# VectorE's middle steps as a loop, and a new order for the last two pairs of K tiles

## The chip, the cores and the metric

The kernel runs on one core of a Trainium2 chip. It uses TensorE (PE, matmul), VectorE (DVE), ScalarE (ACT), GpSimd (POOL, here only for a few set-up instructions and for passing on news of landed transfers) and SyncE (SP, which issues the transfers). The metric is the time of one execution on the device, in microseconds, lower being better. The median of three runs of the kernel before is 2525.35 us (2525.32 to 2525.47).

## The reference, cut to what matters

One token is decoded: attention of one query per head over a long cache (32 heads, 65536 keys, head size 128, bfloat16), a small gated feed-forward block, and a gate that mixes both.

```python
q = (x @ wq).reshape(B, Sq, H, Dh).transpose(0, 2, 1, 3)      # x: 1 x 1 x 512, H = 32, Dh = 128
scores = jnp.einsum("bhqd,bhkd->bhqk", q, k_cache) * (Dh ** -0.5)   # Sk = 65536
p = softmax(scores)
o = jnp.einsum("bhqk,bhkd->bhqd", p, v_cache)
a = o.transpose(0, 2, 1, 3).reshape(B, Sq, H * Dh) @ wo
b = (silu(x @ w_gate) * (x @ w_up)) @ w_down
g = sigmoid((x * gate_w).sum(-1, keepdims=True))
return g * a + (1 - g) * b
```

The K cache and the V cache have 512 MiB each, and every byte of them is read once.

## The kernel before

Keys are handled in *tiles* of 128 x 128 keys: partition p holds 128 keys of 128 numbers, 4 MB in all. A head has four K tiles and four V tiles (G = 4), so there are N = 128 tiles of each, in M = 64 *pairs* (two tiles, 8 MB, half a head). On chip there are two buffers for K pairs (`K_bufs`) and one for a V pair (`V_buf`).

A step m works on K pair m and, two pairs behind it, on V pair m - 2:

- VectorE (`vector_step`) multiplies each K tile by the query, laid out over all partitions (`product`), and adds halves of the 128 columns: 128 to 64, to 32, to 16 (`add_halves`). The last add writes `T_sb`. It also folds finished scores out of PSUM into `S_sb` (`fold`), takes the head's maximum per partition (`row_max`), the maximum over partitions (`top_of`) and the reciprocal of the softmax sum (`weight`).
- TensorE (`tensor_step`) finishes the sum over the remaining 16 columns by matmuls with a unit matrix that accumulate in PSUM, four columns each (`scores`: 16 columns are 4 matmuls, 32 are 8, 64 are 16). It multiplies probabilities by V (`values`, 32 matmuls per tile), turns the head's output (`head_turn`), spreads the query of the next head, turns the maxima (`max_turn`) and sums the exponentials (`total`). Its program already has the middle steps as a loop, in which it waits for *credits*: semaphores that others raise by one and that it lowers again.
- ScalarE (`scalar_step`) takes the exponentials into `P_sb`, spreads queries and scales the head's output.
- SP (`sync_step`) issues the loads: V pair m - 1 when the values of the V pair ahead of it are done (semaphore `pe_V`), for odd pairs as two tiles, and then K pair m + 2 when the scores of pair m are done (`pe_S`). All its transfers go through one queue, in the order in which they are issued.

The first two pairs are written out by hand in `prologue`, 64 columns wide. VectorE, ScalarE and SP have one instruction after the other for all 64 pairs; each waits for counts that only rise, remembered in `seen` so that no count is waited for twice. Order within an engine is the order in which the instructions are written.

At the end there is no more K to load, and the four last V tiles (124 to 127) take the place of what has been used: 124 and 127 lie in halves of the K buffers, 125 and 126 in `V_buf`. The output matrix wo comes in pieces, the first 16 heads early and the rest (`LATE_CUTS`) behind the last V tile. `sync_end` issues all that, `tensor_end` has TensorE's order: scores of the last pair 32 wide, straight from the K buffer (`scores_direct`), values of V tiles 122 to 127, and between them the projection with wo (`project`, two matmuls per head). The last eight columns of the last V tile go straight into `head_turn`'s accumulator. `vector_end` and `scalar_end` copy one half of the output each, and `sync_out` sends it.

Of the kernel before, what the change touches and what calls it, by code (L numbers as in the profile page):

```python
# [10 lines left out]
P = 128  # L11
NB = 128
PAIR = 2 * NB
QUAD = 4

FIRST = 64
WIDTH = 16
LAST = 32

# [22 lines left out]
def kernel(  # L42
# [53 lines left out]
    out_sb = sb("out_sb", [1, D], bf16)  # L96
    qT, rg = sb("qT", [P, H]), sb("rg", [P, H])
    oT = sb("oT", [P, H], bf16)
# [34 lines left out]
    def v_view(n):  # L133
# [8 lines left out]
    )  # L142
    ac, ac_q, dv, dv_top, dv_max, dv_rg = (
        Events(nc, n) for n in ("ac", "ac_q", "dv", "dv_top", "dv_max", "dv_rg")
    )
    x_in, gw_in, wq_in, kb_in, wg_in, wu_in, wd_in, vA_in, vB_in = (
        Events(nc, n, 16)
        for n in ("x_in", "gw_in", "wq_in", "kb_in", "wg_in", "wu_in", "wd_in", "vA_in", "vB_in")
    )
# [9 lines left out]

    seen = {}  # L160

    def wait(engine, events, value):
        key = id(engine), id(events)
        if seen.get(key, 0) < value:
            engine.wait_ge(events.sem, value)
            seen[key] = value
# [33 lines left out]
    def load_k(m):  # L200
        if m in (0, M - 1):
            for n in range(2):
                load_tile(K_half[m % 2][n], A_k_cache, 2 * m + n, (k_in[m % 2], kb_in)[n])
        else:
            load_pair(K_bufs[m % 2], A_k_cache, m, k_in[m % 2])

    def sync_step(m):
        load_v(m - 1)
        if m + 2 < M:
            wait(sync, pe_S, 2 * m + 2)  # L210
            load_k(m + 2)

    def sync_end():
        wait(sync, pe_S, N - 2)
        load_wo(0, EARLY)
        load_tile(v_view(N - 4), A_v_cache, N - 4, v4_in)
        for n in (N - 3, N - 2, N - 1):
            if n < N - 1:
                wait(sync, pe_V, n - 2)
            else:  # L220
                wait(sync, pe_S, N)
            cuts = LAST_CUTS if n == N - 1 else HALVES
            for events, a, b in zip(end_in[n], cuts[:-1], cuts[1:]):
                load_tile(v_view(n), A_v_cache, n, events, a, b)
        for a, b in zip(LATE_CUTS[:-1], LATE_CUTS[1:]):
            load_wo(a, b)

    def sync_out():
        wait(sync, dv, dv.n)
        wait(sync, ac, ac.n)  # L230
        out_in(sync.dma_start(out=out[0], in_=out_sb))
        sync.sem_inc(done.sem, 1)
# [20 lines left out]
    marks = {}  # L253

    def product(n):
        K = K_half[n // 2 % 2][n % 2]
        q = q_sb[n // G % 2]
        q_rep = bass.AP(tensor=q.tensor, offset=q[:, :].offset, ap=[list(q[:, :].ap[0]), [0, NB], [1, Dh]])
        m = n // 2

        if m in (0, M - 1) and n % 2:
            wait(dve, kb_in, 16 if m == 0 else 32)
        else:
            wait(dve, k_in[m % 2], 16 * (m // 2 + 1))
        wait(dve, ac_q, n // G + 1)
        return dv(dve.tensor_tensor(out=K, in0=K, in1=q_rep, op=ALU.mult))  # L266

    def add_halves(n, width, last, out=None, ahead=None):
        K = K_half[n // 2 % 2][n % 2]
        half, mark = Dh // 2, last  # L270
        while half >= width:
            wait(dve, dv, mark)
            to = K[:, :, 0:half]
            if half == width and ahead is not None:
                fold(ahead)
            if half == width and out is not None:
                wait(dve, pe_S, n)
                to = out
            ins = dve.tensor_tensor(out=to, in0=K[:, :, 0:half], in1=K[:, :, half : 2 * half], op=ALU.add)  # L279
            if half == width and out is not None:  # L280
                ins.then_inc(c_S[n % 2], 1)
            else:
                mark = dv(ins)
            half //= 2
        marks["K", n] = mark

    def fold(n):
        h, g = divmod(n, G)
        wait(dve, pe_S, n + 1)
        return dv(dve.tensor_reduce(  # L290
            out=S_sb[h % 2][:, g * NB : (g + 1) * NB], in_=S_ps[n % 2], axis=AXIS.X, op=ALU.add
        ))

    def row_max(h, folded):
        wait(dve, dv, folded)
        dv_max(dve.tensor_reduce(out=m_sb[:, 0:1], in_=S_sb[h % 2], axis=AXIS.X, op=ALU.max))  # L296

    def top_of(h):
        wait(dve, pe_m, 2 * h + 1)
        dv_top(dve.tensor_reduce(out=top[:, 0:1], in_=mT, axis=AXIS.X, op=ALU.max))  # L300

    def weight(h, t):
        wait(dve, pe_t, t)
        if h < H - 1:
            wait(dve, dv, dv(dve.tensor_reduce(out=tsum[:, 0:1], in_=tot, axis=AXIS.X, op=ALU.add)))
            total = tsum[:, 0:1]
        else:
            total = tot[:, 0:1]
        wait(dve, dv, dv(dve.reciprocal(recip[:, 0:1], total)))
        dv_rg(dve.tensor_tensor(out=rg[:, h : h + 1], in0=recip[:, 0:1], in1=gval, op=ALU.mult))  # L310

    def vector_step(m):
        h, b = divmod(m, MH)
        width, to = (WIDTH, T_sb) if m < M - 1 else (LAST, None)
        last = product(2 * m)
# [9 lines left out]
        if b == 1:  # L325
            row_max(h, fold(2 * m + 1))

    def vector_end():
        top_of(H - 1)
        weight(H - 1, M - 1)  # L330
        wait(dve, pe_x, 5)
        dv(dve.tensor_copy(out=out_sb[:, :HD], in_=a_ps[0]))  # L332

# [4 lines left out]
    def query(h, credit):  # L338
# [7 lines left out]
        wait(act, pe_q, pe_q_after(2 * h - 1) if h else 1)  # L346
        ac_q(copy(q_sb[h % 2], qb))

# [4 lines left out]
    def head_diag(h, credit):  # L353
        m = 2 * h + 1
        wait(act, dv_max, h + 1)
        wait(act, pe_m, m - 1)
        ins = copy(diag, ident_f, m_sb[:, 0:1])
# [25 lines left out]
    def head_out(h, src):  # L383
        wait(act, dv_rg, h + 1)
        if h >= GROUPED:
            return copy(oT[:, h : h + 1], src, rg[:, h : h + 1])
        g, part = divmod(h, QUAD)
        A = P // QUAD
        for j in range(QUAD):
            ins = copy(  # L390
                oT[part * A : (part + 1) * A, g * QUAD + j : g * QUAD + j + 1],
                src[j * A : (j + 1) * A, :],
                rg[j * A : (j + 1) * A, h : h + 1],
            )
# [31 lines left out]
    def scalar_end():  # L426
# [12 lines left out]
        wait(act, pe_x, 6)  # L439
        ac(copy(out_sb[:, HD:], a_ps[1]))  # L440

# [4 lines left out]

    def scores(n, src, width):
        for c in range(0, width, QUAD):
# [3 lines left out]
            )  # L452
        pe_S(ins)

    def scores_direct(n, width):
        wait(pe, dv, marks["K", n])
        scores(n, K_half[n // 2 % 2][n % 2], width)

    def query_spread():
        pe_q(pe.matmul(qb, lhsT=ones_b, rhs=q_diag, start=True, stop=True))  # L460

    def max_turn():
        pe_m(pe.matmul(mT, lhsT=ones_f, rhs=diag, start=True, stop=True))  # L463

# [30 lines left out]
    def prologue():  # L495
# [35 lines left out]

        add_halves(0, FIRST, product(0))
        scores_direct(0, FIRST)
        wait(dve, x_in, 16)
# [8 lines left out]
        fold(0)  # L543
        add_halves(1, FIRST, last)
        scores_direct(1, FIRST)
        wait(dve, ac, marks["eg2"])
# [18 lines left out]
        marks["eg"] = ac(act.activation(out=eg, in_=gu_sb[:, :FT], func=ACT.Exp, scale=-1.0))  # L565
        wait(sync, pe_S, 2)
        load_k(2)

        last = product(2)
        fold(1)  # L570
        add_halves(2, FIRST, last)
        scores_direct(2, FIRST)
        wait(dve, ac, marks["eg"])
# [24 lines left out]
        fold(2)  # L598
        add_halves(3, FIRST, last)
        scores_direct(3, FIRST)  # L600
        wait(sync, pe_S, 4)
        load_k(3)
        row_max(0, fold(3))
        head_diag(0, False)
        wait(pe, ac, marks["diag", 0])
        max_turn()


    def tensor_step():
# [4 lines left out]
        take(c_S[0])  # L614
        scores(0, T_sb, WIDTH)
        take(c_q)
# [3 lines left out]
        take(c_S[1])  # L620
        scores(1, T_sb, WIDTH)
        take(c_o)
        head_turn()
        take(c_m)
        max_turn()

    def tensor_end():
        scores_direct(N - 2, LAST)
        take(c_P)
        total()  # L630
        take(c_V)
        pe_V(values(P_sb, V_half[0], 0, NB, True, False))
        take(c_V)
        lower = P_sb[:, NB:]
        values(lower, V_half[1], 0, NB // 2, False, False)
        scores_direct(N - 1, LAST)
        values(lower, V_half[1], NB // 2, 3 * NB // 4, False, False)
        wait(pe, ac, marks["diag", H - 1])
        max_turn()
        pe_V(values(lower, V_half[1], 3 * NB // 4, NB, False, True))  # L640
        wait(pe, wo_in[0], 16)
# [18 lines left out]
        for j in range(NB - TURNED, NB):  # L660
# [3 lines left out]
            )  # L664
        wait(pe, ac, marks["O_last"])
        head_turn(opens=False)
        for a, b in zip(LATE_CUTS[:-1], LATE_CUTS[1:]):
            wait(pe, wo_in[a], 16)
            if b == H:
                project(a, H - 1)  # L670
# [5 lines left out]
    with tc.tile_critical():  # L676
        prologue()
        for m in range(2, M):
            vector_step(m)
            scalar_step(m)  # L680
# [3 lines left out]
        sync_end()  # L684
        scalar_end()
        vector_end()
        sync_out()
        with pe.Fori(0, M - 3):
            tensor_step()
# [38 lines left out]
```

## Time and profile before

| | |
|---|---|
| median of 3 runs | 2525.35 us |
| the profiled execution: time / span | 2523.84 us / 2522.0 us |
| DMA: bytes, mean rate | 1087.85 MB, 431 GB/s |
| busy: PE / VectorE / ScalarE | 55% / 88% / 7% of the span |
| TensorE's mean granted clock | 0.731 |
| product of a K tile (line 266), 128 times | 8.69 us each |
| add to 64 columns / to 32 / to 16 (line 279) | 4.42 / 2.29 / 1.22 us |
| fold of a tile (line 290) | 0.69 us |
| values matmul (line 470), 3968 in the middle steps | 0.42 us each, mean |

The span runs from the first to the last instruction of the profiled execution; the 1.84 us around it belong to the execution's own time. Times in the views count from the span's start. A line such as `DVE K_buf L266 <- DMA K_buf: 148.7, 57, 5.6` says that VectorE stood idle ahead of instructions of line 266 until a transfer into a K buffer landed, 148.7 us in total, 57 times, 5.6 us at most. In the timeline a row has its start, its length, the engine, the line, the operation, what it writes and reads, and in brackets the engine's idle time ahead of it. The view of DMA issues gives, for each kind of transfer, how many, their size and the median time from issue to landing.

### The profile page before, as it was taken

The page shows a single profiled execution, that of the slowest core. Times are in us where ns is not written, and L with a number is a line of the kernel's source. Part 1 is how long each engine was busy: PE and PEld are TensorE (multiplying, and loading weights), DVE is VectorE, ACT ScalarE, POOL GpSimd, SP SyncE. Part 2 cuts the span into 40 slices and gives each one's busy share as a digit, 9 for nine tenths or more (in the row PEclk, how much of TensorE's full clock was granted, in tenths as well). Part 3 has the DMA queues.
Part 4 walks back from the last instruction along what each step waited for, and adds up shares of the span by engine and source line. Part 5 has one row for each costly group of instructions (what it writes and reads, how often), then busy time and mean ns, then how long its engine had stood idle before and what let it go on. Part 6 is the DMA issues. An engine that isn't in the chain of part 4 may idle for free. (4 is left out here: it accounts for less than half of the span.)

```text
span 2522.0 us, 14146 instructions
## 1 busy us (share of the span) xinstructions
PE 1388.8 (55%) x5813; PEld 574.9 (23%) x5813; DVE 2220.4 (88%) x802; ACT 187.2 (7%) x503; POOL 0.7 (0%) x6
## 2 busy tenths in 40 slices
PE   2655654546645465554565454654545555556549
PEld 1222222212212122222222121222212222222214
DVE  5898898988988989889889898898898988988992
ACT  0000000000000000000000000000000000000000
POOL 0000000000000000000000000000000000000000
PEclk9767776767767677676777676776767767677769
DMA  9999999999999999999999999999999999999998
GB/s 414 437 435 433 434 439 429 440 433 432 432 432 434 435 432 437 439 428 439 432 433 432 432 437 432 434 437 434 430 439 433 432 433 433 434 432 435 439 429 348
DMA packets 26854, 1087.85 MB, mean 431 GB/s; under 512 B 3154, under 2 KB 3667, under 8 KB 4947
## 3 DMA queue, kind: packets, MB, share of 16 engines
q1 hardware_dynamic: 26546, 1087.65, 99.7%
q8 instruction: 5, 0.08, 0.0%
q14 instruction: 15, 0.11, 0.0%
q10 hardware_dynamic: 288, 0.00, 0.0%
HBM read 1087.64 MB, written 0.00 MB: 431 GB/s over the span
## 5 line engine op out<-in xcount | busy, mean ns | idle before, releaser
L470 PE MATMUL O_ps<-V_buf,P_sb 128*4 128x512 bf16 x3968 | 1006.7, 418 | 519.6 <-PEq L445 519.3
L266 DVE TENSOR_TENSOR K_buf<-K_buf,q_sb 128x16384 bf16<-128x16384 bf16 x128 | 1112.0, 8688 | 173.5 <-DMA K_buf<-in_A_k_cache_dram 173.5
L279 DVE TENSOR_TENSOR K_buf<-K_buf 128x8192 bf16<-128x8192 bf16 x252 | 849.7, 3372 | 5.3
L470 PEld LDWEIGHTS O_ps<-V_buf,P_sb 128*4 128x4 bf16 x3968 | 353.7, 91 | 1132.4 <-issue 729.9
L449 PE MATMUL S_ps<-T_sb,ident_b 128*128 128x512 bf16 x488 | 156.3, 449 | 240.0 <-PEq L445 240.0
L466 PE MATMUL tot_ps<-rs,ones_f 128*128 128x2 f32 (+1 forms) x126 | 29.1, 300 | 230.7 <-PEq L445 230.7
L290 DVE TENSOR_REDUCE S_sb<-S_ps 128x128 f32<-128x512 f32 x128 | 88.3, 690 | 71.8 <-PE S_ps L449 69.7
L279 DVE TENSOR_TENSOR T_sb<-K_buf 128x2048 bf16<-128x2048 bf16 x122 | 148.8, 1220 | 2.1
L336 ACT ACTIVATE O_sb<-O_ps 4x512 f32<-4x512 f32 x63 | 63.0, 1000 | 1066.0 <-PE O_ps L470 1066.0
L449 PEld LDWEIGHTS S_ps<-T_sb,ident_b 128*128 128x128 bf16 x488 | 41.0, 103 | 335.9 <-issue 311.4
L478 PEld LDWEIGHTS oh_ps<-ident_f,O_sb 4*128 4x128 f32 x504 | 85.9, 253 | 46.6 <-issue 46.1
L478 PE MATMUL oh_ps<-ident_f,O_sb 4*128 4x1 f32 x504 | 90.5, 296 | 6.1 <-PEq L445 5.7
L466 PEld LDWEIGHTS tot_ps<-rs,ones_f 128*128 128x128 f32 x126 | 25.7, 254 | 244.5 <-issue 244.4
L463 PE MATMUL qm_ps<-diag,ones_f 128*128 128x128 f32 x126 | 38.5, 398 | 69.7 <-PEq L445 67.6
L449 PE MATMUL S_ps<-K_buf,ident_b 128*128 128x512 bf16 x80 | 27.6, 515 | 44.0 <-DVE K_buf L279 35.7
L336 ACT ACTIVATE q_sb<-qm_ps 128x128 bf16<-128x128 f32 x32 | 8.9, 278 | 560.5 <-PE qm_ps L460 560.5
L463 PEld LDWEIGHTS qm_ps<-diag,ones_f 128*128 128x128 f32 x126 | 25.1, 249 | 74.1 <-issue 71.0
L336 ACT ACTIVATE oT<-whole_o,rg 32x1 bf16<-32x1 f32 (+1 forms) x115 | 33.8, 294 | 2.0
L399 ACT ACTIVATE whole_o<-oh_ps,half_o 128x1 f32<-128x1 f32 x31 | 8.1, 261 | 317.9 <-PE oh_ps L478 317.9
L368 ACT ACTIVATE P_sb<-S_sb,bias 128x256 bf16<-128x256 f32 x62 | 31.5, 508 | 1.2 <-issue 0.2
L332 DVE CAST out_sb<-a_ps 1x256 bf16<-1x256 f32 x1 | 0.4, 413 | 27.0 <-PE a_ps L487 27.0
L449 PEld LDWEIGHTS S_ps<-K_buf,ident_b 128*128 128x128 bf16 x80 | 9.4, 123 | 60.0 <-DVE K_buf L279 45.0
(60 smaller groups left out, 200.4 us busy)
## 6 DMA issues: line engine op xcount, KB each, us to landing
V_buf<-in_A_v_cache_dram SPq DMA_DIRECT2D x62, 4096.0 KB, 20.4
K_buf<-in_A_k_cache_dram SPq DMA_DIRECT2D x4, 4096.0 KB, 31.4
V_buf<-in_A_v_cache_dram SPq DMA_DIRECT2D x4, 2048.0 KB, 17.6
V_buf<-in_A_wq_dram SPq DMA_DIRECT2D x1, 4096.0 KB, 12.4
K_buf<-in_A_v_cache_dram SPq DMA_DIRECT2D x1, 4096.0 KB, 34.1
K_buf<-in_A_v_cache_dram SPq DMA_DIRECT2D x3, 1024.0 KB, 23.3
K_buf<-in_A_wo_dram SPq DMA_DIRECT2D x1, 2048.0 KB, 24.9
V_buf<-in_B_w_gate_dram SPq DMA_DIRECT2D x1, 1792.0 KB, 54.4
```

Of the source, the lines that this page charges most:

```text
L266: return dv(dve.tensor_tensor(out=K, in0=K, in1=q_rep, op=ALU.mult))
L279: ins = dve.tensor_tensor(out=to, in0=K[:, :, 0:half], in1=K[:, :, half : 2 * half], op=ALU.add)
L290: return dv(dve.tensor_reduce(out=S_sb[h % 2][:, g * NB : (g + 1) * NB], in_=S_ps[n % 2], axis=AXIS.X, op=ALU.add))
L332: dv(dve.tensor_copy(out=out_sb[:, :HD], in_=a_ps[0]))
L336: return act.activation(out=out, in_=in_, func=ACT.Copy, scale=scale)
L368: return act.activation(out=out, in_=S_sb[h % 2][:, b * PAIR : b * PAIR + count], func=ACT.Exp, bias=bias[:, 0:1], scale=scale, accum_out= ...
L399: wait(act, ac, ac(act.activation(out=whole_o[:, 0:1], in_=oh, func=ACT.Identity, bias=half_o[:, 0:1], scale=1.0)))
L449: ins = pe.matmul(S_ps[n % 2], lhsT=ident_b, rhs=src[:, :, c : c + QUAD], start=(c == 0), stop=(c == width - QUAD),)
L463: pe_m(pe.matmul(mT, lhsT=ones_f, rhs=diag, start=True, stop=True))
L466: pe_t(pe.matmul(tot[:, :n], lhsT=ones_f, rhs=rs[:, :n], start=True, stop=True))
L470: ins = pe.matmul(O_ps, lhsT=probs[:, j : j + 4], rhs=view[:, j : j + 4, :], start=(opens and j == start), stop=(closes and j == stop - 4),)
L478: ins = pe.matmul(oh, lhsT=O_sb[:, c * Dh : (c + 1) * Dh], rhs=ident_f[0:4, c : c + 1], start=(opens and c == 0), stop=(c == 3),)
```

## The change

- **A loop on VectorE.** Pairs 2 to 61 become 15 rounds of four pairs (`vector_round`, two heads). Within a round the waits count from the round's start; at its end VectorE waits for what the round's counts must have reached and lowers each semaphore by as much. `own[0]` says which counter VectorE's own instructions raise, in the loop `dv_loop`. Counters that the loop lowers are waited for by VectorE alone, so others get their own: the scores of the hand-written pairs raise `pe_D`, first loads of K raise `ka_in`, `kb_in` and `kc_in`, the first query raises `ac`. `rg` has two columns instead of 32.
- **K loads wait for another event.** SP issues K pair m + 2 after step m's `head_turn` (`pe_o`), where it was after its scores (`pe_S`). ScalarE's `head_diag` no longer waits for `pe_m`.
- **The last two pairs**, 62 and 63, stand outside both loops (TensorE's runs 60 times, not 61), and both are 64 columns wide: one add per tile on VectorE, 16 matmuls per tile on TensorE, where pair 62 was 16 and pair 63 was 32 wide.
- **TensorE's order at the end.** In both last steps the scores of a tile stand ahead of the values of a tile: scores 124, values 120, scores 125, values 121, then scores 126, values 122, scores 127, values 123 in two halves with the max turn between. The last `head_turn` moves behind the first four heads of the 16-to-24 piece of wo, for which TensorE thus waits earlier.

```diff
-        width, to = (WIDTH, T_sb) if m < M - 1 else (LAST, None)
+        width, to = (WIDTH, T_sb) if m < M - 2 else (WIDE, None)
...
+    def vector_round():
+        own[0] = dv_loop
+        for m in range(2, 2 + 2 * MH):
+            vector_step(m)
+        for events, n in ((dv_loop, dv_loop.n), (pe_S, 8), (pe_m, 4), (pe_t, 4), (ac_q, 2), *((k, 32) for k in k_in)):
+            dve.wait_ge(events.sem, n)
+            dve.sem_inc(events.sem, -n)
+        own[0] = dv
...
     def sync_step(m):
         load_v(m - 1)
         if m + 2 < M:
-            wait(sync, pe_S, 2 * m + 2)
+            wait(sync, pe_o, m - 1)
             load_k(m + 2)
 
     def sync_end():
-        wait(sync, pe_S, N - 2)
+        wait(sync, pe_D, 6)
         load_wo(0, EARLY)
...
-                wait(sync, pe_S, N)
+                wait(sync, pe_D, 8)
...
     def head_diag(h, credit):
-        m = 2 * h + 1
         wait(act, dv_max, h + 1)
-        wait(act, pe_m, m - 1)
...
     def tensor_end():
-        scores_direct(N - 2, LAST)
+        lower = P_sb[:, NB:]
         take(c_P)
         total()
+        scores_direct(N - 4)
         take(c_V)
         pe_V(values(P_sb, V_half[0], 0, NB, True, False))
+        scores_direct(N - 3)
+        take(c_q)
+        query_spread()
         take(c_V)
-        lower = P_sb[:, NB:]
+        pe_V(values(lower, V_half[1], 0, NB, False, True))
+        take(c_o)
+        head_turn()
+        take(c_m)
+        max_turn()
+
+        take(c_P)
+        total()
+        scores_direct(N - 2)
+        take(c_V)
+        pe_V(values(P_sb, V_half[0], 0, NB, True, False))
+        scores_direct(N - 1)
+        take(c_V)
         values(lower, V_half[1], 0, NB // 2, False, False)
-        scores_direct(N - 1, LAST)
-        values(lower, V_half[1], NB // 2, 3 * NB // 4, False, False)
         wait(pe, ac, marks["diag", H - 1])
         max_turn()
-        pe_V(values(lower, V_half[1], 3 * NB // 4, NB, False, True))
+        pe_V(values(lower, V_half[1], NB // 2, NB, False, True))
...
-        wait(pe, ac, marks["O_last"])
-        head_turn(opens=False)
         for a, b in zip(LATE_CUTS[:-1], LATE_CUTS[1:]):
             wait(pe, wo_in[a], 16)
-            if b == H:
+            if a == EARLY:
+                project(a, a + QUAD)
+                wait(pe, ac, marks["O_last"])
+                head_turn(opens=False)
+                project(a + QUAD, b)
+            elif b == H:
                 project(a, H - 1)
...
         for m in range(2, M):
-            vector_step(m)
             scalar_step(m)
...
-        with pe.Fori(0, M - 3):
+        with dve.Fori(0, (M - 4) // (2 * MH)):
+            vector_round()
+        vector_end()
+        with pe.Fori(0, M - 4):
             tensor_step()
```

## The prediction

> **What bounds the kernel now.** I read the page's DMA slices and queues first, then the stretches, the DMA issues with their time to landing, and last the timeline of the end.
>
> ```profile
> DMA  9999999999999999999999999999999999999998
> DMA packets 26854, 1087.85 MB, mean 431 GB/s; under 512 B 3154, under 2 KB 3667, under 8 KB 4947
> q1 hardware_dynamic: 26546, 1087.65, 99.7%
> q8 instruction: 5, 0.08, 0.0%
> q14 instruction: 15, 0.11, 0.0%
> ```
>
> The one queue that SP issues on keeps the 16 DMA engines busy for 99.7% of the span. VectorE is 88% busy, but it waits for DMA: in the waits of VectorE between 90 and 2400 us the first row is
>
> ```profile
> DVE K_buf L266 <- DMA K_buf<-in_A_k_cache_dram: 148.7, 57, 5.6
> ```
>
> Those 2310 us are 14.8 stretches of four pairs (four pairs move 67 MB, 155 us at 433 GB/s), so VectorE has 148.7 / 14.8 = 10 us to spare in each four pairs. How far the transfers are issued ahead is read from the DMA issues:
>
> ```profile
> V_buf<-in_A_v_cache_dram SPq DMA_DIRECT2D x62, 4096.0 KB, 20.4
> K_buf<-in_A_v_cache_dram SPq DMA_DIRECT2D x1, 4096.0 KB, 34.1
> K_buf<-in_A_wo_dram SPq DMA_DIRECT2D x1, 1024.0 KB, 28.4
> K_buf<-in_A_k_cache_dram SPq DMA_DIRECT2D x62, 40.3
> V_buf<-in_A_v_cache_dram SPq DMA_DIRECT2D x31, 30.9
> gwT<-in_gate_w_dram ACTq DMA_DIRECT2D x1, 1.0 KB, 14.4
> ```
>
> A 4 MB tile takes 9.7 us and an 8 MB pair 19.4 us at that rate. A V tile lands 20.4 us after its issue, so it lay about 10.7 us behind other transfers; a V pair 30.9 - 19.4 = 11.5 us; a K pair 40.3 - 19.4 = 20.9 us. The DMA runs dry only where an issue is later than that. So the time is the stream of bytes plus what follows its end, and the end is in TensorE's timeline:
>
> ```profile
> 2475.63 1.90 PE L449 MATMUL S_ps<-K_buf,ident_b 128*128 128x512 bf16 x8 [1.33 <-DVE K_buf L279]
> ...
> 2484.43 7.07 PE L470 MATMUL O_ps<-K_buf,T_sb 128*4 128x512 bf16 x32
> ...
> 2493.49 13.98 PE L470 MATMUL O_ps<-V_buf,T_sb 128*4 128x512 bf16 x64
> 2507.30 6.64 PE L470 MATMUL O_ps<-K_buf,T_sb 128*4 128x512 bf16 x30
> 2513.87 0.35 PE L661 MATMUL oh_ps<-T_sb,K_buf 128*128 128x1 bf16 x8
> 2514.61 1.05 PE L478 MATMUL oh_ps<-ident_f,O_sb 4*128 4x1 f32 x8 [0.39 <-ACT O_sb L336]
> 2515.59 3.65 PE L487 MATMUL a_ps<-K_buf,oT 128*1 128x256 bf16 x32
> ```
>
> From 2484.4 us TensorE hardly stops until 2519.2 us, and 2.8 us of output follow (2522.0). The transfers end just ahead of it: V tile 124 was issued at 2447.91 and landed 34.1 us later, at 2482.0; the 1 MB piece of wo was issued at 2485.50 and landed 28.4 us later, at 2513.9; the last piece of wo was issued at 2502.55 and landed 13.9 us later (the source view of line 189), at 2516.45.
>
> **The change, part by part.**
>
> *VectorE's loop.* Same vector instructions for pairs 2 to 61; each of 15 rounds adds seven waits, seven decrements, a register step and a branch. All seven waits are for counts that an instruction earlier in the round has already waited for, so they hold nothing up. No loop of VectorE is in this trace. TensorE's is: at its turn the last matmul of a step ends at 1053.77 and the first weight load of the next starts at 1053.95, 0.2 us. From below: 0. From above: if the round's start had to fetch code, a small transfer under a busy DMA costs up to the 14.4 us of gwT (1 KB). I take 1 us, as TensorE's turn is the nearest row: 0.2 us, and 14 short instructions, estimated at the 0.06 us of this trace's shortest vector instruction (the memset of line 514). 1 us a round is hidden by the 10 us to spare: 0.
>
> [...]
>
> *K loads wait for pe_o, not pe_S.* SP issues K pair m+2 after the head turn of step m instead of after its scores. In the timeline at 1012 us: scores end 1012.38, K issued 1012.40, head turn ends 1014.16. So 1.8 us later, out of a lead of 20.9 us. Behind this wait on SP stands the V load of the next step, which waits for values that come some 28 us later (1014 to 1042.8). Cost 0; the cover fails from 20 us.
>
> *ScalarE's dropped wait on pe_m, rg with two columns, out_a/out_b for the output.* No time: ScalarE is 7% busy, and the output's copies are the last of their engines as before.
>
> *Last two pairs 64 wide.* VectorE drops four half-size adds of 2.29 us and two final adds of 1.22 us: 11.6 us. TensorE does 64 score matmuls for the last four tiles instead of 4+4+8+8 = 24. At the fast rate (16 values matmuls 3.5 us, 0.22 us each) 40 more are 8.7 us; at the slow rate (8 in 3.6 us at 2459 us, clock 0.50) up to 18 us.
>
> *The new order, worked through.* VectorE: K pair 62 landed at 2409.3; with 1 us for the loop's end, product 8.7, top 0.3, add 4.4, product 8.7, fold 0.7, add 4.4 reach 2437.5. Tile 126's K is in at 2438.3 (the 30.8 us of its load); product 8.7, fold 0.7, add 4.4 end at 2452.1; product, weight, fold, add (8.7 + 0.5 + 0.7 + 4.4) at 2466.4. Before, the last add ended at 2475.6.
> TensorE: scores 124 from 2424, some 7 us at the slow clock, done before V pair 60 lands at 2428.6 + 3. Values 60A to 2439; scores 125 3.5; query and values 60B 7.4: 2450. ScalarE's copy, head turn, max turn, exponentials, total: some 3.5 us, 2453.5. Scores 126 to 2457; V tile 122 lands at 2457.7, values 61A to 2464.8; scores 127 from 2466.4 to 2469.9 (before: 2477.5). From there to V tile 124 it has 32 values matmuls (7.0), the max turn (0.5), 16 projections (1.9), a head turn (1.0): 10.4 us, so 2480.3, and V tile 124 lands at 2482.0. Before, it began at 2484.4. The 40 added matmuls are thus paid out of VectorE's 11.6 us and TensorE's idle stretches, and the wait that is late next is a transfer.
>
> SP's issues stay ahead of the stream: V tile 122 at 2439 (was 2438.4), 123 at 2450 (2446.5, lead about 11 us), wo and 124 at 2451, 125 at 2465 (was 2470.9). DMA does not run dry.
>
> *From 2482 to the end.* TensorE's values run 2.4 us earlier, as far as transfers allow: the last values end at about 2511.9 instead of 2513.9. Then the new order asks for the 1 MB piece of wo, landed 2513.9, ahead of the head turn. Behind it: eight projections, the head turn 1.05 (its copy is long done), 24 more projections; 3.65 + 1.05 = 4.7 us: 2518.6 instead of 2519.2.
>
> **Sum: -0.7 us**, nothing before 2482 counted. Bounds: if TensorE came no earlier at all, the copy (0.4 us of wait) would still be covered by projections, less what they are in the way: -0.25. If only the last piece of wo bounded, 2516.45 + four projections 0.5 + output 2.8 = 2519.7: -2.3. The profiled execution took 2523.84 us (span 2522.0 and 1.84 around it) and is 1.5 us below the median of 2525.35; -0.7 off the median is 2524.6.
>
> **Rivals.**
>
> 1. *TensorE is late at the end.* For it: 40 more matmuls, and the clock is 0.50 after each idle stretch. Against: it has 1.7 us to spare before V tile 124 and is 4.1 us ahead of before. If all 48 score matmuls after 2428 ran at the slow rate it would be 48 x 0.23 = 11 us later than my 2480.3, 2491, 6.9 us behind the old 2484.4: 2525.35 + 6.9 - 0.25 = 2532. Half of them: 2526.5. It passes 0.2% from some 9 us of delay.
>
> 2. *The loop's turn fetches code.* Its place is VectorE's first instruction of each round. Priced by the landing of gwT, 14.4 us, against 10 us to spare: 4.4 us x 15 = 66 us, 2591. It decides from 10 us a turn (and at xT's 2.3 us, before the queues filled, costs nothing). Against: TensorE's 0.2 us a turn. [...]
>
> 3. *The stream itself changes speed.* K issues come 1.8 us later, and nothing says how the engines pack them. Four stretches of 600 us show 434, 433, 434, 433 GB/s; 0.5 GB/s is 0.12%, 2.9 us either way: 2522.5 to 2528.3. A gain of over 5 us needs 0.9 GB/s.
>
> **How the numbers follow.** Forecast 0.79, with its own range 2523.0 to 2525.6; rival 1 0.11 (0.03 of it over 0.2%); rival 2 0.05 (0.04 over 0.2%); rival 3 0.05 (0.03 faster, 0.01 slower by over 0.2%). 0.2% is 5 us, about what a measurement of this kernel tells from no change: faster 0.03, same 0.89, slower 0.08. The range goes a little below the stream's bound for rival 3 and above for half of rival 1: 2522.8 to 2527.5.
>
> **What would show it.** Right: DMA again 99% or more on one queue; VectorE's wait for K about 10 us a round with no new gap at a round's start; K pairs landing about 38.5 us after issue; V tile 124's values starting as it lands, with TensorE waiting for it; a wait for wo ahead of the last head turn; end 0 to 2 us earlier. Wrong: a gap of several us at every 155 us on VectorE, DMA slices below 9, or V tile 124's values starting after 2484 without a wait.

## The result, and the profile after

The kernel after takes 2520.03 us (median of 18 executions, 2519.74 to 2523.24) where the kernel before, beside it, takes 2525.26 us (18 executions, 2523.70 to 2525.48). The ratio is 0.9983, with a 95% interval of 0.9976 to 0.9989. The forecast was 2524.6 us with a range down to 2522.8, so it came out too high. The profiled executions are 2523.84 us (span 2522.0) and 2520.16 us (span 2518.4), 3.7 us apart.

The page of the kernel after, its DMA part:

```profile
DMA  9999999999999999999999999999999999999998
q1 hardware_dynamic: 26546, 1087.65, 99.8%
q8 instruction: 6, 0.10, 0.0%
q14 instruction: 8, 0.07, 0.0%
```

The data queue carries the same 26546 packets. What differs is the instruction packets. That they bring the compute engines' code the runs below show: 372, 1116 and 2232 more instructions on GpSimd made 11, 17 and 25 packets on q14 out of the 8 here. On q14 there are 8, each of 8 KB, where there were 15, of which 14 had 8 KB and one, at the start, 88 bytes. On q8 there are 6 packets of 16 KB instead of 5; they are put down to TensorE, whose program has one more step outside its loop. VectorE's waits between 90 and 2400 us:

```profile
DVE K_buf L279 <- DMA K_buf<-in_A_k_cache_dram: 137.3, 43, 5.1
DVE K_buf L279 <- DVEq L351: 8.0, 14, 1.1
```

The second row is the loop's turn: 14 turns, 0.57 us on average, 1.1 us at most. VectorE still waits 137.3 us for K, so the turns are hidden, as forecast. TensorE's timeline of the end:

```profile
2463.00 3.63 PE L483 MATMUL S_ps<-K_buf,ident_b 128*128 128x512 bf16 x16 [0.63 <-DVE K_buf L291]
...
2479.13 8.42 PE L504 MATMUL O_ps<-K_buf,T_sb 128*4 128x512 bf16 x32 [2.26 <-DMA K_buf<-in_A_v_cache_dram]
...
2489.54 13.98 PE L504 MATMUL O_ps<-V_buf,T_sb 128*4 128x512 bf16 x64
2503.35 6.64 PE L504 MATMUL O_ps<-K_buf,T_sb 128*4 128x512 bf16 x30
...
2510.88 1.03 PE L521 MATMUL a_ps<-K_buf,oT 128*1 128x256 bf16 x8 [0.60 <-DMA K_buf<-in_A_wo_dram]
2511.84 1.05 PE L512 MATMUL oh_ps<-ident_f,O_sb 4*128 4x1 f32 x8
2512.82 2.78 PE L521 MATMUL a_ps<-K_buf,oT 128*1 128x256 bf16 x24
```

TensorE now waits 2.26 us for V tile 124 and 0.60 us for the piece of wo ahead of the last head turn. Against the landing of the last piece of wo the end moved little: it landed at 2516.45 before and at 2513.46 after, and the span ended 5.55 us and 4.94 us behind it. So of the 3.6 us of span, **3.0 us are the stream of transfers, which ended earlier, and 0.6 us the new end.**

Where the stream gained is found by following its landings. In both traces a pair lands 19.31 to 19.33 us after the one before, with a few exceptions, each of which makes everything behind it late: before, by 0.41, 0.95, 0.98, 0.96, 0.98 and 0.97 us (at 511, 879, 1247, 1596, 1964 and 2293 us), 5.25 us together; after, by 0.20, 0.67 and 0.66 us (at 1265, 1758 and 2271 us), 1.53 us together. Of this difference of 3.7 us 3.0 are left at the last landing: the stream after already lies 0.3 us behind at 200 us, and some 0.4 us are spread over many landings. The DMA view between 845 and 900 us shows one of them. First the kernel before, then the kernel after (its columns are packets, MB and share for a queue, and median us to landing at the end of an issue):

```profile
q14 instruction: 1, 0.01, 0.0%
...
K_buf<-in_A_k_cache_dram SPq DMA_DIRECT2D x2, 40.3
V_buf<-in_A_v_cache_dram SPq DMA_DIRECT2D x1, 32.3
```

```profile
q1 hardware_dynamic: 433, 23.30, 97.8%
...
K_buf<-in_A_k_cache_dram SPq DMA_DIRECT2D x2, 38.8
V_buf<-in_A_v_cache_dram SPq DMA_DIRECT2D x1, 31.3
```

The V pair, issued within 0.03 us of the same time in both, lands 32.3 us later with an instruction packet among the data and 31.3 us later without one. Each late landing follows such a packet by some us. The packets one by one, around the one at 507.2 us of the kernel before (queue, start us, length ns, bytes):

```
q1  506.735  2418  65536
q14 507.204   309   8192
q1  507.510  2948  65536
q1  507.652  2418  65536
```

The code packet takes 0.31 us on its DMA engine, and the data packet that starts as it ends takes 2948 ns instead of 2418: 0.84 us in all. The records don't name the DMA engine; following which packet starts where another ended puts all code of one compute engine, other than TensorE's, on one DMA engine (in the trace after, ScalarE's packets at 255, 775, 1249, 1753 and 2256 us). By when they come, VectorE has 7 of these packets within the stream before (168, 507, 863, 1243, 1592, 1948 and 2290 us) and one after; ScalarE has 5 in both, SP and GpSimd one each. As built, VectorE's program shrank from 910 instructions to 130, and one packet holds about 130 of them (below, 2232 more instructions bring 17 more packets).

### The profile page after: what moved, and what is told of

It is laid out like the page before. It is cut to its first block, busy times and chain, and to the rows that moved or that the text cites. A ratio compares the mean times of both kernels' runs of the same rounds, so it can differ in the third digit from the quotient of the medians.

```text
span 2518.4 us, 14321 instructions
## 1 busy us (share of the span) xinstructions
PE 1398.6 (56%) x5853; PEld 578.9 (23%) x5853; DVE 2209.0 (88%) x796; ACT 187.3 (7%) x503; POOL 0.7 (0%) x6
## 3 DMA queue, kind: packets, MB, share of 16 engines
q1 hardware_dynamic: 26546, 1087.65, 99.8%
## 5 line engine op out<-in xcount | busy, mean ns | idle before, releaser
L291 DVE TENSOR_TENSOR K_buf<-K_buf 128x8192 bf16<-128x8192 bf16 x248 | 840.6, 3390 | 5.2
L483 PE MATMUL S_ps<-K_buf,ident_b 128*128 128x512 bf16 x128 | 41.3, 491 | 38.6 <-DVE K_buf L291 30.3
L483 PEld LDWEIGHTS S_ps<-K_buf,ident_b 128*128 128x128 bf16 x128 | 14.5, 119 | 63.1 <-DVE K_buf L291 40.2
```

Source lines behind the costliest of these rows:

```text
L483: ins = pe.matmul(S_ps[n % 2], lhsT=ident_b, rhs=src[:, :, c : c + QUAD], start=(c == 0), stop=(c == width - QUAD),)
```

## The experiments

Three theories stood at the start. *Code fetching*: the loop's program is short, so fewer code packets delay the stream. *Packing*: the later K issues change how the stream runs (the prediction's rival 3). *The end*: the new order is worth more than 0.7 us.

### Only the loop undone

```diff
-        with dve.Fori(0, (M - 4) // (2 * MH)):
+        for _ in range((M - 4) // (2 * MH)):
             vector_round()
+            for events in (dv_loop, *looped):
+                seen.pop((id(dve), id(events)), None)
+            dv_loop.n = 0
```

VectorE gets the 15 rounds one after the other, 1008 instructions, with the same waits and decrements.

> The changed kernel with VectorE's 15 rounds written out (same instructions, waits and decrements, no branch). Theory of code fetches: in the two traces each 8 KB instruction packet holds up the one DMA engine that carries it (VectorE's by 0.31 us and another 0.53 us on the next data packet, ScalarE's by 0.31 + 0.25), each engine of the core has its code fetched by one DMA engine, and the stream lands with the DMA engine that is furthest behind, less the 1.4 us that TensorE's first code packets put on other DMA engines. VectorE again needs about 8 packets on one DMA engine, 6.7 us, where ScalarE's 5 now set 2.8: about 3.9 us slower than the changed kernel's 2520.0, 2523.9 (2525.4 where its DMA engine also carried a packet of TensorE). Rival, that the gain lies in the later K issue, the new end or the loop's own timing: no change, 2520.0 within 0.5.

Measured: 2524.34 us (10 executions, 2523.90 to 2527.36), 4.3 us above the kernel after, so the loss is back with all else of the change in place. The page's code queue and VectorE's waits:

```profile
q14 instruction: 15, 0.12, 0.0%
```

```profile
DVE K_buf L279 <- DMA K_buf<-in_A_k_cache_dram: 144.7, 43, 5.6
DVE K_buf L279 <- DVEq L351: 5.6, 14, 0.4
```

Landings are late seven times, by 0.37 and six times 0.95 to 0.99 us, and the last one is at 2517.62 us, 4.2 us later than with the loop. Unrolled, VectorE's program is longer than the 910 instructions before the change, with 8 code packets instead of 7, so that a little more comes back than the loop brought. The row of the turn shows what the loop itself costs: 0.57 us a turn with the branch and 0.40 us with the same waits and no branch.

### Only the end, and only the K issue

The kernel before with the new end (last two pairs 64 wide, TensorE's new order, no loop on VectorE):

```diff
-        width, to = (WIDTH, T_sb) if m < M - 1 else (LAST, None)
+        width, to = (WIDTH, T_sb) if m < M - 2 else (FIRST, None)
...
     def tensor_end():
-        scores_direct(N - 2, LAST)
...
+            if a == EARLY:
+                project(a, a + QUAD)
+                wait(pe, ac, marks["O_last"])
+                head_turn(opens=False)
+                project(a + QUAD, b)
```

> The kernel before with the new end alone: pairs 62 and 63 64 columns wide, TensorE's new order, 60 turns of its loop; no loop on VectorE, K issue as before. Theory of code fetches: VectorE still fetches 7 packets, the stream lands as before, and only the end is shorter, by the 0.7 us of the prediction: 2524.6 against 2525.3. Rival, that the end brings the whole gain: 2520.

Measured: 2523.32 us (10 executions; nine between 2522.95 and 2524.03, one at 2526.40), span of the profiled one 2521.3. The six late landings are there as before (last landing 2516.36 us). Against the profiled execution before the end is worth 0.7 us of span, as forecast; against the median beside it (2525.14 us) 1.8 us, which the two values below explain. What the loop adds to it is 2520.03 - 2523.32 = -3.3 us.

The kernel before with K loads waiting for the head turn:

```diff
-            wait(sync, pe_S, 2 * m + 2)
+            wait(sync, pe_o, m - 1)
             load_k(m + 2)
```

> The kernel before with one line changed: SP waits for the head turn instead of the scores ahead of each K load. Theory of code fetches: K issues some 1.8 us later inside a lead of 21 us, nothing else, 2525.3 within 0.3. Rival, that the other times of issue let the DMA engines pack better: 3 us faster, 2522.

Measured: 2524.55 us, five executions at 2523.59 to 2523.89 and five at 2525.22 to 2525.46. The kernel before has the same two values (beside it, 25 executions: 11 from 2523.68 to 2524.03, 14 from 2525.11 to 2525.80). So the K issue does nothing, and packing falls.

The kernel before was profiled once more, for those two values:

> The kernel before again, for a second trace, because its times fall on two values, 2523.8 and 2525.4. Theory of code fetches: if this execution takes 2525.4, its trace shows VectorE's code on a DMA engine that was already behind by one code packet of TensorE, some 1.4 us, and the stream landing that much later; if it takes 2523.8, the two are on different DMA engines. Rival, some other cause: the same places of the packets in both.

It fell on the lower value, 2523.82 us, with the packets and late landings of the first profile, so it could not tell. The trace of the K-issue kernel, an execution of 2525.36 us, could. Its stream ends as in the first profile, within 0.2 us; what differs comes ahead of the scores of tile 127. Its timeline and, below, its window (length, then busy us of PE, PEld, DVE, ACT and POOL, granted clock, DMA share, GB/s):

```profile
2475.49 3.58 PE L449 MATMUL S_ps<-K_buf,ident_b 128*128 128x512 bf16 x8 [2.55 <-DVE K_buf L279]
```

```profile
2476.00:2480.00 4.00, 4.00 (x13) 1.20 (x12) 0.86 (x2) 0.00 (x0) 0.00 (x0) 0.64 0.97 418
```

and the same window of the kernel before (2523.84 us):

```profile
2476.00:2480.00 4.00, 3.88 (x19) 1.46 (x17) 1.38 (x3) 0.40 (x1) 0.00 (x0) 1.00 0.96 414
```

TensorE stood still for 2.55 us instead of 1.33, its granted clock over the next 4 us was 0.64 instead of 1.00, and the eight score matmuls took 3.58 us instead of 1.90. All of TensorE's work behind is 1.5 us later. The stop was longer because TensorE had been faster ahead of it: its clock from 2460 to 2464 us was 0.77 against 0.50, and its 48 values matmuls took 10.52 us against 11.25, while the add of VectorE that it then waits for ended within 0.2 us of the same time. That the stop makes the two values is tested below.

### More code packets on GpSimd

If a code packet costs time whoever fetches it, idle instructions on GpSimd must cost it too. They go into `tell_of_v`, once per step, with k = 3, 9 and 18:

```diff
+        for _ in range(k):
+            pool.sem_inc(idle_sem, 1)
+            pool.sem_inc(idle_sem, -1)
```

GpSimd raises and lowers a semaphore that no one reads. Two versions of the theory differ: either every packet costs by itself, or the stream lands with the DMA engine that is furthest behind, so that only the compute engine with the costliest packets counts.

> The changed kernel with code added on GpSimd alone, which is idle: 6 instructions a step that raise and lower a semaphore nobody reads, 372 in all, three more code packets of 8 KB. Theory that the stream waits for the DMA engine furthest behind: GpSimd's 4 packets cost 4 x 0.53 = 2.1 us on their DMA engine, less than ScalarE's 5 x 0.555 = 2.8, so no change, 2520.0 within 0.3. Rival, that every packet costs the stream its own time: 3 x 0.53 = 1.6 us slower, 2521.6. Rival, that code fetches have nothing to do with it: 2520.0 here and in the next two.

> The same with 18 instructions a step, 1116 in all, some nine code packets more. DMA engine furthest behind: GpSimd's 9 to 10 packets put theirs 4.7 to 5.3 us behind, 2.0 to 2.5 us more than ScalarE's 2.8: 2522.0 to 2522.5. Every packet for itself: 8.7 x 0.53 = 4.6 us slower, 2524.6. No part of code fetches: 2520.0.

> The same with 36 instructions a step, 2232 in all, some 17 code packets more. DMA engine furthest behind: 18 to 18.4 x 0.53 = 9.6 us, 6.8 more than ScalarE's 2.8: 2526.8, and 4.6 us over the run with nine. Every packet for itself: 9.2 us slower, 2529.2. No part of code fetches: 2520.0.

The code queue on the three pages:

```profile
q14 instruction: 11, 0.09, 0.0%
```

```profile
q14 instruction: 17, 0.14, 0.0%
```

```profile
q14 instruction: 25, 0.20, 0.0%
```

| k | packets on q14 | last landing, us | median, us (range) |
|---|---|---|---|
| 0 (the kernel after) | 8 | 2513.46 | 2520.03 (2519.74 to 2523.24) |
| 3 | 11 | 2513.66 | 2520.20 (2519.76 to 2523.23) |
| 9 | 17 | 2515.54 | 2522.67 (2522.26 to 2523.34) |
| 18 | 25 | 2520.82 | 2527.77 (2526.85 to 2529.79) |

Three packets more cost nothing (0.2 us), nine cost 2.6 us and the seventeen that k = 18 brings 7.7 us; a packet of GpSimd shifts the landings by 0.62 to 0.67 us each time it counts. The sum over all packets asked for 2521.6, 2524.6 and 2529.2 us, and all three runs lie below it; "furthest behind" asked for 2520.0, 2522.0 to 2522.5 and 2526.8, and they lie 0.2 to 1.0 us above that. So here one packet was not added to another when they sat on different DMA engines. The landings say the same: with k = 9 all six late ones, from 975 to 2253 us, follow a packet of GpSimd, and ScalarE's packets at 1249, 1753 and 2258 us, which made landings late in the kernel after, delay nothing.

What is free at first is seen in all of them: 7 x 0.97 = 6.8 us for VectorE's packets before, of which 5.25 show; 8 x 0.97 = 7.8 of which 6.2 show when unrolled; 5 x 0.66 = 3.3 for ScalarE's after, of which 1.53 show. Some 1.5 to 1.8 us are lost in each. The three packets of 16 KB at 19, 69 and 110 us, put down to TensorE and 0.88 to 0.96 us long, lie on three other DMA engines in the trace after, by following packets as above; that they put those behind first fits but was not tested.

### The order of the last head turn undone

```diff
+        wait(pe, ac, marks["O_last"])
+        head_turn(opens=False)
         for a, b in zip(LATE_CUTS[:-1], LATE_CUTS[1:]):
             wait(pe, wo_in[a], 16)
-            if a == EARLY:
-                project(a, a + QUAD)
-                wait(pe, ac, marks["O_last"])
-                head_turn(opens=False)
-                project(a + QUAD, b)
-            elif b == H:
+            if b == H:
```

> The changed kernel with one thing of the end undone: the last head turn ahead of all projections with the late pieces of wo, as it was. In the changed kernel's trace TensorE waits 0.6 us for the 1 MB piece of wo, then has eight projections, the head turn, 24 projections. With the head turn first it fills that wait: the copy it needs ends at 2510.6, head turn 1.05 to 2511.7, 32 projections 3.65 to 2515.4 instead of 2515.6: 0.2 us faster, 2519.8. If the last landings of wo rule instead: the same, 2520.0. If projecting first were right: 0.3 us slower.

Measured: 2519.10 us (11 executions, 2518.66 to 2521.18), ratio to before 0.9979 (0.9970 to 0.9988). That part of the change was a small loss, 0.9 us and not the 0.2 expected. If TensorE is early enough, it turns the head while the 1 MB piece of wo is still in flight, and the 1.05 us of the turn no longer follow that landing; the first trace of the section on work in place of the wait shows it so (head turn at 2509.86, projections at 2511.02 us). The profiled execution here was the slowest of the eleven, and in it the head turn came after the landing (2510.63 us):

```profile
2478.93 9.94 PE L504 MATMUL O_ps<-K_buf,T_sb 128*4 128x512 bf16 x32 [2.27 <-DMA K_buf<-in_A_v_cache_dram]
...
2511.98 1.05 PE L512 MATMUL oh_ps<-ident_f,O_sb 4*128 4x1 f32 x8 [0.39 <-ACT O_sb L368]
2512.96 3.65 PE L521 MATMUL a_ps<-K_buf,oT 128*1 128x256 bf16 x32
```

The 32 matmuls of V tile 124 took 9.94 us here, 8.42 in the kernel after and 7.07 before, where TensorE had not waited ahead of them. Of the other ten executions seven lie from 2518.66 to 2519.18 and three from 2519.83 to 2520.01; that they differ by how long the matmuls were slow would fit, but was not shown.

### Less code on ScalarE

ScalarE's packets now set the stream's loss. In the kernel of the last section, the four scaled copies of each early head move to GpSimd, and ScalarE's program goes from 580 to 440 instructions:

```diff
-            ins = copy(
+            ins = pool.tensor_tensor(
                 oT[part * A : (part + 1) * A, g * QUAD + j : g * QUAD + j + 1],
```

> The run with the last head turn first, and in addition the four copies that scale each of the heads 0 to 27 into oT moved from ScalarE to GpSimd: ScalarE's program falls from 580 to 440 instructions (about 1.1 code packets of 8 KB fewer), GpSimd's grows from 120 to 260 (about one more). DMA engine furthest behind: ScalarE's 4 packets instead of 5 (or 3), at the 0.66 us by which each of the last ones moved the stream's landings in the changed kernel's trace: 0.7 us faster (1.2 if 3) than the run with the head turn first, 2518.4 against 2519.1; GpSimd's 2 packets stay behind that. Every packet for itself: no change in their number, 2519.1. If GpSimd's copies got in the way of VectorE or were late for the end: slower than 2519.1.

Measured: 2519.39 us (11 executions, 2518.51 to 2519.71), no lower than 2519.10. The stream did what was expected of it: only two late landings, 0.27 and 0.68 us, and the last at 2512.84 us instead of 2513.25. But the end did not follow:

```profile
2478.54 8.75 PE L517 MATMUL O_ps<-K_buf,T_sb 128*4 128x512 bf16 x32 [2.26 <-DMA K_buf<-in_A_v_cache_dram]
...
2510.41 1.05 PE L525 MATMUL oh_ps<-ident_f,O_sb 4*128 4x1 f32 x8 [0.39 <-ACT O_sb L368]
```

TensorE no longer waits for wo (its 1 MB landed at 2510.26, while TensorE was still to turn the head). Its own work from V tile 124 on is the bound, and that begins with slow matmuls.

### Work in place of the wait

Ten matmuls, whose results go to a score buffer that is no longer read, fill the 2.3 us in which TensorE waits for V tile 124; first in the kernel with the head turn first, then in the one with less code on ScalarE:

```diff
         wait(pe, ac, marks["P_last"])
+        for _ in range(10):
+            pe.matmul(S_ps[0], lhsT=ident_b, rhs=P_last.rearrange("p (k c) -> p k c", c=QUAD), start=True, stop=True)
         wait(pe, v4_in, 16)
```

> e7_order with ten matmuls into a score buffer that is no longer read, issued while TensorE waits for V tile 124 (their results are not used). Theory (the granted clock falls because TensorE stood still for 2.3 us, and the first matmuls behind pay for it): the 32 matmuls of tile 124 take 7.1 to 7.3 us instead of 8.4 (in the kernel after) to 9.9 (in e7_order), with the clock near 1.0; then the last piece of wo bounds the end, 2513.25 us + 0.5 to 0.8 + 2.8 + 1.8 around the span: 2518.5 us against 2519.1. Rival (these matmuls are slow because the tile they read has only just landed, or for another reason of the place): 8.4 us or more again, and 2519.1 us or a little above.

> The same ten matmuls in e9_less_act. Theory: the 1.5 us that TensorE lost there come back and the stream's earlier end shows: last landing 2512.84 + 0.5 to 0.8 + 2.8 + 1.8 = 2518.0 to 2518.3 us, against 2519.4 without them. Rival: 2519.4 us.

Measured: 2518.99 us (11 executions, 2518.64 to 2519.59) and 2518.67 us (11 executions, 2518.08 to 2519.30). Timeline and window of the first of them, then the same window of the kernel after:

```profile
2476.94 2.33 PE L696 MATMUL S_ps<-T_sb,ident_b 128*128 128x512 bf16 x10
2479.20 7.07 PE L504 MATMUL O_ps<-K_buf,T_sb 128*4 128x512 bf16 x32
...
2511.02 3.65 PE L521 MATMUL a_ps<-K_buf,oT 128*1 128x256 bf16 x32
```

```profile
2480.00:2482.00 2.00, 2.00 (x11) 0.77 (x9) 0.00 (x0) 0.00 (x0) 0.00 (x0) 1.00 1.01 434
```

```profile
2480.00:2482.00 2.00, 2.00 (x7) 0.58 (x6) 0.00 (x0) 0.00 (x0) 0.00 (x0) 0.53 1.01 434
```

The clock stays at 1.00 instead of falling to 0.53, and the 32 matmuls take 7.07 us in both new kernels. So with the stop filled the clock stayed, and the matmuls' time goes with the clock. But the stop does not always bring the fall: with k = 3 on GpSimd TensorE waited as long, its clock from 2480 to 2482 us was 1.00, and the matmuls took 7.07 us. In the seven other traces in which TensorE waited for this tile, by 2.2 to 2.9 us, they took 8.4 to 9.9 us.

```profile
2479.34 7.07 PE L508 MATMUL O_ps<-K_buf,T_sb 128*4 128x512 bf16 x32 [2.27 <-DMA K_buf<-in_A_v_cache_dram]
...
2511.08 1.03 PE L525 MATMUL a_ps<-K_buf,oT 128*1 128x256 bf16 x8 [1.55 <-DMA K_buf<-in_A_wo_dram]
```

In this trace, which has the new order of the kernel after, the fast matmuls only made the wait for the 1 MB piece of wo longer, 1.55 us instead of 0.60. From the end of that wait to the end of the last projection it is 4.72 us in both. So the slow matmuls cost the kernel after no time; they count where the head turn comes first.

The times gained less than expected, 0.1 and 0.7 us instead of 0.6 and 1.1 to 1.4, because the next bound was named wrongly: not the last piece of wo but the 1 MB piece. It landed at 2510.97 us; the projections start at 2511.02 and their 32 matmuls of 3.65 us run on to the end. The second kernel, in which it landed at 2510.50, is the fastest of all, ratio to before 0.9977 (0.9968 to 0.9986).

The same remedy in the kernel before, against the stop ahead of the scores of tile 127:

```diff
+        for _ in range(11):
+            pe.matmul(
+                S_ps[1][:, : 2 * NB // QUAD, :], lhsT=ident_b,
+                rhs=P_sb.rearrange("p (k c) -> p k c", c=QUAD), start=True, stop=True,
+            )
         scores_direct(N - 1, LAST)
```

> The kernel before with eleven half-width matmuls (1.2 us at the full clock, results not used) ahead of the scores of tile 127, where TensorE stood still for 1.33 us in the execution of 2523.8 us and for 2.55 us in that of 2525.4. Theory (the two values are this stop with and without a fall of the clock): the stop is at most 1.3 us, the clock stays, and all executions lie at the lower value, 2523.6 to 2524.2 us. Rival (the two values come from elsewhere): about half of the executions at 2525.2 to 2525.5 again.

Measured: 2523.89 us (11 executions): nine from 2523.51 to 2524.53, and one each at 2524.84 and 2525.21. Beside it the kernel before had 14 executions up to 2524.22 and 13 from 2525.10 up. The stop is 0.30 us in its profile:

```profile
2475.86 1.91 PE L449 MATMUL S_ps<-K_buf,ident_b 128*128 128x512 bf16 x8 [0.30 <-DVE K_buf L279]
```

Two of eleven above 2524.8 us where the kernel before had 13 of 27 fits the stop as the cause of most of the upper value. It is not the cause of all: with the clock alone as cause, no execution should lie at 2525.2.

## Why the prediction was wrong

- **"nothing before 2482 counted".** This is the step that failed. The stream before that point was taken as fixed by its bytes, with VectorE's loop costed at 0 from both its sides, 0 and 14.4 us a round. The loop had a gain in another place: 6 code packets fewer on the DMA engine that had been furthest behind, and a stream that ends 3.0 us earlier. Undoing the loop alone gives 4.3 us back; the loop on top of the new end gives 3.3 us.
- **The instruction packets.** The lines `q8 instruction: 5` and `q14 instruction: 15, 0.11, 0.0%` stood in the first fence, and no term of the sum was made of them. Their share of 0.0% is an average over 16 DMA engines. 7 packets of VectorE are 2.2 us on one of them, 5.9 us with the longer data packets behind them, and each transfer is spread over the engines and lands with its last part: in the trace before 16 packets of the data queue run at once for 96% of the time from 200 to 2400 us, and each transfer has 16 landings, of which the last ends the wait. A bound, "a gain of at most 7 packets of some us of one engine", could have been set from that line.
- **Code as a wait at the loop's turn.** The prediction priced a fetch of code only there, from above with gwT's 14.4 us, and took 1 us a turn after TensorE's 0.2. The turn is 0.57 us, 1.1 at most, and VectorE has one code packet within the stream, at 168 us. The price of its code was in the DMA, the bound here: 0.97 us a packet, after the first 1.5 us.
- **Rival 3, "The stream itself changes speed".** It had the place and the size: 2.9 us either way, and 3.0 came. Its mechanism, K issues packed in another way, fell: that edit alone changes nothing. So its chance of 0.05 was for a reason that was not the one.
- **"-0.7 off the median is 2524.6".** The 0.7 was right: 0.6 in the trace after, 0.7 of span with the new end alone. But the profiled execution was on the lower of two values of the kernel before and the median on the upper, and with the new end, which moves the scores of tile 127 out of the place of that stop, nine of ten executions lie together. Subtracting from the median left 1.5 us standing that went. The miss of 4.6 us is these 1.5 us and the stream's 3.0.
- **The end, step by step.** TensorE "at 2480.3, and V tile 124 lands at 2482.0": TensorE was early and waited, 2.26 us. What the sum did not have is that the 32 matmuls behind this wait took 8.42 us instead of 7.07. That did no harm to its result: the end is bound by the landing of the 1 MB piece of wo, and the 4.7 us that the sum put behind it are 4.72 in the trace. With stops of 2.2 to 2.9 us these matmuls were slow in seven traces, 8.4 to 9.9 us; with one of 2.27 us (k = 3) they took 7.07 us, and behind the stop of 1.33 us in the kernel before the clock was 1.00 (2476 to 2480 us).
- **"The new order asks for the 1 MB piece of wo ... ahead of the head turn".** It waits 0.60 us there, as forecast. That this is no gain was in the forecast's bounds (-0.25 to -2.3) only as a smaller gain; the old order, with all else new, is 0.9 us faster.
- **Rivals 1 and 2** did not come: TensorE was not late, and VectorE has no code packet after the one at 168 us. Its turn, taken as 1 us, is 0.57 us and hidden as said. Rival 1's "the clock is 0.50 after each idle stretch" holds for the steps at 1008 to 1036 and 2452 to 2464 us, not for the stop of 1.33 us, nor for the one of 19.35 us ahead of 37.49 us (clock 1.00 from 36 to 44 us).

Open: a few executions lie some 3 us above the rest (2523.24 of the kernel after, 2523.23 with k = 3, 2527.36 and 2527.29 unrolled, 2526.40 with the new end alone). None of them was profiled. It is also open why the clock fell with most stops of some 2.3 us and not with one of them. Nor is it settled why the data packet behind a code packet takes longer, or which part of the 0.97 us is not in the 0.84 us of the two packets.

## What to carry to other kernels

In this kernel, whose data queue kept the 16 DMA engines busy for 99.8% of the span, the length of a program was part of the stream. So count the instructions of each engine, and look for the one whose code packets put its DMA engine furthest behind. The loop on that engine was worth 4.3 us although VectorE had some 10 us to spare in each round; three more code packets on GpSimd, which was not the furthest behind, cost 0.2 us, and six more on top 2.5. A stop of TensorE of 2.26 us was followed by a clock of 0.53 and 32 matmuls of 8.42 us instead of 7.07. Ten matmuls in its place, whose result is not used, kept the clock at 1.00, and gained 0.1 and 0.7 us: work in place of a stop is worth trying where TensorE's own time, and not a transfer, bounds what follows.

## What the runs showed of the hardware

- An 8 KB code packet, 0.31 us long, made every later landing of a busy stream late by 0.95 to 0.99 us when it was VectorE's, 0.66 to 0.69 when it was ScalarE's, 0.62 to 0.67 when it was GpSimd's, once the DMA engine that carried it was the one furthest behind; the first 1.5 to 1.8 us did not show. Packets of different compute engines did not add up: with 17 on q14 the time was 2522.67 us, where the sum asked for 2524.6.
- With a TensorE stop of 2.2 to 2.9 us ahead of V tile 124, 32 matmuls took 8.4 to 9.9 us instead of 7.07 in seven traces (granted clock 0.53 over 2 us in the kernel after) and 7.07 in an eighth (clock 1.00). With a stop of 2.55 us eight matmuls took 3.58 us instead of 1.90 (clock 0.64 over 4 us). With the stop filled, the clock stayed at 1.00 in both traces.
- A round's end on VectorE with its seven waits and seven decrements took 0.40 us (5.6 us in 14, unrolled), and 0.57 us with the loop's branch (8.0 us in 14).
